# Two attention branches on one core: local projections first, attention blocks spread over two stages, the gate on column tiles, the range test read late

## The chip, the cores and the metric

The kernel runs on one core of a Trainium2 chip. The metric is device time in microseconds (us) of one execution, and fewer is better. Five engines run their own instruction streams: PE (TensorE, matmuls, with its weight loads listed as PEld), DVE (VectorE), ACT (ScalarE), POOL (GpSimd) and SP (SyncE, which here only issues DMAs). PE writes to PSUM, eight banks of 128 x 512 f32 values; ACT and DVE read it out.

## The reference

Two branches read the same x (2048 x 1024) and are mixed by a gate per row. H is 32 heads of 32 columns.

```
g = sigmoid((x * gate_w).sum(-1, keepdims=True))
# A, linear attention:   q, k, v = split(x @ A_wqkv)
phi = lambda t: where(t > 0, t + 1, exp(t)) + 1e-6
kv = phi(k)^T v (32 x 32 per head);   z = sum over rows of phi(k)
a = ((phi(q) @ kv) / (phi(q) @ z + 1e-6)) @ A_wo
# B, local attention:    q, k, v = split(x @ B_wqkv)
each row attends to itself and the 7 rows 2, 4, ... 14 before it, softmax
b = (softmax(q k^T / sqrt(32)) @ v) @ B_wo
out = g * a + (1 - g) * b
```

## The kernel before, in words

Even and odd rows of x are kept apart (the local window steps by two), so that a window is 8 neighbouring rows of one parity. `xT` holds x transposed, 8 slices of 128 features by 2048 rows, in 16 row tiles of 128. Every projection is made of groups: eight matmuls 128x128 by 128x512, one for each feature slice, into one PSUM bank (`group`, L1237). There are 256 groups in all, 2048 such matmuls. `ws` holds four weight slots of 1024 columns (in the profile w_4, w_5, w_6, w_7 for slots 0 to 3), loaded in halves of 512 columns (`load_w`, L1208).

The order of the instructions comes from a planner, `Prog`. Each operation is recorded with its engine, an estimated cost, what it reads and writes, and a priority (by default its place in the program). `schedule` places the operations by these costs, on each engine always the ready one with the lowest priority number, and `emit` writes the five streams in that order with semaphore waits. On the chip each engine then runs its stream strictly in order. PSUM banks are handed out in rotation (`Ring.next`) in program order, before the planner moves anything: a group must wait until the bank it was given has been read out.

The stages of before, in program order:

1. Linear k and v (L1257 to L1291): for each of 16 row tiles four groups. The first also computes the gate's sum with eight extra 128x1 matmuls (L1280). phi on k is three operations (`phi_natural`: ACT Exp L1247, DVE min and add L1248, DVE max and add L1250), v is one ACT copy (L1289). Then 32 small matmuls on column tiles (L1262) add the tile's kv and z into bank 7, which stays open for the whole stage. Six banks rotate.
2. Local v (L1310 to L1324): 32 groups, read out through two `vst` tiles and stored to DRAM, from where the attention blocks load their windows.
3. Fold (L1334 to L1352): the block-diagonal kv is transposed in eight steps and multiplied into A_wo in 16 matmuls, so that later one product with `ws[3]` does both. Three banks rotate.
4. Local k and q (L1418 to L1446): 64 groups, all read out by DVE (L1440, L1442), and 2 x 2 running maxima for the range test (`top`, L1194). From the second quarter on, `slot(0.36)` lets an attention block in about every third group. There are 36 blocks (`fill`). A block is 16 score matmuls on row tiles into banks 4 to 7 (L1380), one Exp on ACT (E, L1385), the mask on DVE (L1388), and two groups later 32 matmuls on column tiles: values into bank 3 and sums into a rotating bank (L1398, L1402); ACT makes Ln and Exp of the sums (L1407, L1408), DVE multiplies (L1409). Only banks 0, 1 and 2 rotate for everything else.
5. Linear q, the numerators (L1455 to L1473): 32 groups with phi and a running maximum; two slots later (`over`) the denominator matmul (L1465), Ln and Exp on ACT (L1467, L1468) and a product on DVE (L1470). Attention blocks go on in between, and three banks still rotate.
6. A's output (L1480 to L1492): 32 groups with the folded weights, read out into the same place, scaled by g (L1489). The last blocks lie in between.
7. The range test (L1496 to L1511): the maxima go through DRAM and back (L1502, L1503) to one partition, and `flag` says whether the fast formulas were safe. Every engine reads it at its very end.
8. B's output (L1515 to L1528): 32 groups, combined on DVE and stored.

Of the kernel before, what the change touches and what calls it, by code (L numbers as in the profile page):

```python
# [24 lines left out]
class Tile:  # L25
# [13 lines left out]
    def all(self):  # L39
        return [(self.space, self.lo, self.lo + self.row * self.size)]  # L40

    def part(self, *idx):
# [12 lines left out]
        return [(self.space, b + lo * self.size, b + hi * self.size) for b in out]  # L55
# [6 lines left out]
class Prog:  # L62
# [14 lines left out]
    def op(self, eng, fn, cost, reads=(), writes=(), prio=None, chan=None, lat=0.0, after=(), name=""):  # L77
# [10 lines left out]
        for sp, lo, hi in rd:  # L88
# [7 lines left out]
        for sp, lo, hi in wr:  # L96
            for rec in self.recs.get(sp, ()):
                if rec[0] < hi and lo < rec[1]:
                    o.deps.add(rec[2])
        o.deps.discard(o)  # L100
        for sp, lo, hi in wr:
            lst = self.recs.setdefault(sp, [])
            lst[:] = [r for r in lst if not (lo <= r[0] and r[1] <= hi)]
            lst.append((lo, hi, o, True))
        for sp, lo, hi in rd:
            self.recs.setdefault(sp, []).append((lo, hi, o, False))
# [59 lines left out]
    def emit(self, block, tail):  # L166
# [8 lines left out]
        for o in order:  # L175
# [891 lines left out]
def build_kernel(nc, A_x, A_wqkv, A_wo, B_x, B_wqkv, B_wo, gate_w, out):  # L1067
# [37 lines left out]
    class Bank:  # L1105
        def __init__(self, i):
            self.i = i
            self.iv = [("P", i, i + 1)]
# [6 lines left out]
    MX = [("M", 0, 1)]  # L1115
    mx_hbm = nc.dram_tensor("mx_hbm", [4, 128], F32)

    def hb(p0, p1):
        return [("H", p0, p1)]
# [13 lines left out]
    gm = SB([128, NT], F32, "gm")  # L1133
    kvbd = SB([128, 8, 128], BF16, "kvbd")
    zbd = SB([128, 8, 128], BF16, "zbd")
    mx = [SB([128, 512 if i == 2 else 1024], BF16, "mx%d" % i) for i in range(3)]
    mx4 = SB([128, 4], F32, "mx4")
    mx1 = SB([1, 4], F32, "mx1")
    flag = SB([1, 1], I32, "flag")
    er = Ring([SB([128, 512], BF16, "e%d" % i) for i in range(3)])  # L1140
    ph = base[0]

    pk = Ring([SB([128, 1024], BF16, "pk%d" % i) for i in range(2)])
    az = Ring([SB([128, H, 33], BF16, "az%d" % i) for i in range(2)])
    vst = Ring([SB([128, 1024], BF16, "vst%d" % i) for i in range(2)])
    top = base[0]

# [4 lines left out]
    base[0] = max(base[0], top)  # L1152
    pr = Ring([SB([128, 512], BF16, "p%d" % i) for i in range(3)])
    kvT = SB([128, 8, 128], BF16, "kvT", at=pr.t[0].lo)
    mxr = SB([1, 4, 128], F32, "mxr", at=pr.t[0].lo)
    RAr = Ring([SB([128, 512], F32, "ra%d" % i) for i in range(2)])
    osb = Ring([SB([128, 1024], BF16, "o%d" % i, at=RAr.t[i].lo) for i in range(2)])
    if base[0] > nc.sbuf_usable_end:
        raise ValueError("SBUF %d over" % (base[0] - nc.sbuf_usable_end))

    mm = lambda n: max(n / 2400.0, 0.0267) + 0.0025
# [25 lines left out]
    for m in mx:  # L1187
        C("dve", lambda e, m=m: e.memset(m[:, :], 0.0), 0.2, [m.all()])

    def top(ms, src, reg, n):  # L1190

        for i, op in zip(ms, (ALU.max, ALU.min)):
            m = mx[i]
            P.op("dve", lambda e, m=m, op=op: e.tensor_tensor(m[:, 0:n], m[:, 0:n], src, op), 0.06 + n / 1920.0, reads=[m.all(), reg], writes=[m.all()])  # L1194
# [7 lines left out]
    def load_x(t, prio):  # L1202
        e_, r = t // 8, t % 8
        return P.op("sp", lambda e: e.dma_start_transpose(xT[:, :, t * 128:(t + 1) * 128], x2[e_, r * 128:(r + 1) * 128, :]),
                    0.3, writes=[xT.part((0, 8), (t * 128, (t + 1) * 128))], prio=prio, chan="x%d" % t, lat=1.3)

    def load_w(slot, half, src, c0, prio, n=512):
        return P.op("sp", lambda e: e.dma_start(ws[slot][:, :, half * 512:half * 512 + n], src[:, :, c0:c0 + n]), 1.4 * n / 512,  # L1208
                    writes=[ws[slot].part((0, 8), (half * 512, half * 512 + n))], prio=prio, chan="w%d_%d" % (slot, half), lat=4.5 * n / 512)
# [6 lines left out]
    load_w(0, 0, Aw, 1024, 1)  # L1216
    P.op("sp", gw_load, 0.6, writes=[gw.all()], prio=1.5, chan="gw", lat=0.5)
    load_w(0, 1, Aw, 1536, 2)
    load_w(1, 0, Aw, 2048, 3)
    load_x(1, 3.5)  # L1220
    load_w(1, 1, Aw, 2560, 4)
    for t in range(2, NT):
        load_x(t, 3 + t)
    load_w(2, 0, Bw, 2048, 20)
    load_w(2, 1, Bw, 2560, 21)
    load_w(3, 0, Ao, 0, 30)
    load_w(3, 1, Ao, 512, 31)
# [357 lines left out]
```

## Time and profile before

| what | value |
|---|---|
| median of 3 runs | 562.78 us (561.68 to 563.06) |
| the profiled execution's own time | 562.65 us |
| its span, first to last instruction | 560.7 us |
| mean granted TensorE clock | 0.98 |
| PE, DVE, ACT busy | 92%, 54%, 36% of the span |

The profile's views give times from the span's start. Busy time of PE is modelled for pipelined matmuls, so two of its figures are of use: start to start of matmuls that follow one another, and stretches where it is not busy at all. A stretch table has, for each engine, its busy time and in brackets its instruction count, then the granted clock, the busy share of the 16 DMA engines and the rate.

### The profile page before, as it was taken

What the parts mean: (1) busy time and instruction counts of PE and PEld (TensorE: products, weight loads), DVE (VectorE), ACT (ScalarE), POOL (GpSimd) and SP (SyncE); (2) the same over time, 40 slices, a digit from 0 to 9 for tenths busy, and PEclk for the clock granted to TensorE, in tenths of its full rate; (3) what the DMA queues carried; (4) which work ended last, traced back from release to release, by engine and by line L of the source; (5) the groups of instructions that cost most, each with busy time, mean ns of one, the idle gap of its engine ahead of it and who ended that gap; (6) DMA issues with size and microseconds to landing.
All of it is one profiled execution on the core that took longest, in us unless ns stands there. A gap on an engine that the chain in (4) does not pass through costs nothing.

```text
span 560.7 us, 10080 instructions
## 1 busy us (share of the span) xinstructions
PE 514.2 (92%) x4472; PEld 230.9 (41%) x4472; DVE 303.4 (54%) x514; ACT 202.5 (36%) x294; POOL 4.7 (1%) x21
## 2 busy tenths in 40 slices
PE   3999999999999789999999998888884999999996
PEld 1444444444444234444444443333331333444443
DVE  1222222224211347788888899888882555634443
ACT  1233232332111210133443469888882355300000
POOL 3000000000000000000000000000000000000000
PEclk9999999999999979999999999999998899999999
DMA  8997000009312600002100030000000011001222
GB/s 242 223 197 240 1 1 2 1 1 305 127 75 76 205 0 1 1 20 95 29 21 20 20 106 11 9 11 20 11 11 10 21 30 29 1 2 68 83 76 78
DMA packets 44948, 34.81 MB, mean 62 GB/s; under 512 B 19809, under 2 KB 40801, under 8 KB 44898
## 3 DMA queue, kind: packets, MB, share of 16 engines
q1 hardware_dynamic: 44898, 34.09, 21.1%
q8 instruction: 37, 0.61, 0.4%
q14 instruction: 13, 0.11, 0.1%
HBM read 21.50 MB, written 8.39 MB: 53 GB/s over the span
## 4 chain that ended last, share of the span: by engine, by line
PE 81%; DVE 8%; ACT 5%; DMA 4%; SPq 1%; issue 1%
PE ps_all L1237 75%; DMA mx_hbm<-mx_22_70 2%; DMA w_5_53<-in_A_wqkv_dram 2%; PE ps_all L1398 2%; PE ps_all L1343 1%; PE ps_all L1380 1%; PE ps_all L1402 1%; PE ps_all L1262 1%; DVE xT_49 L1489 1%; ACT w_7_55 L1349 1%; ACT ra_48_96 L1467 1%; ACT ra_48_96 L1468 1%; DVE xT_49 L1470 1%; DVE p_43_91 L1250 1%; DVE p_44_92 L1250 1%
## 5 line engine op out<-in xcount | busy, mean ns | idle before, releaser
L1237 PE MATMUL ps_all<-w_4_52,xT_49 128*128 128x512 bf16 x256 | 62.5, 383 | 9.7 <-DMA gw_61<-in_gate_w_dram 9.7
L1237 PE MATMUL ps_all<-xT_49,w_6_54 128*128 128x512 bf16 x256 | 60.5, 380 | 9.2 <-ACT ra_48_96 L1467 2.8
L1237 PE MATMUL ps_all<-xT_49,w_4_52 128*128 128x512 bf16 x256 | 59.7, 385 | 0.0
L1237 PE MATMUL ps_all<-w_5_53,xT_49 128*128 128x512 bf16 x256 | 58.0, 380 | 0.8 <-DMA w_5_53<-in_A_wqkv_dram 0.8
L1237 PE MATMUL ps_all<-xT_49,w_5_53 128*128 128x512 bf16 x256 | 58.6, 379 | 0.0
L1237 PE MATMUL ps_all<-w_4_52,qT_50 128*128 128x512 bf16 x256 | 55.9, 379 | 0.4 <-ACT E_36_84 L1385 0.4
L1237 PE MATMUL ps_all<-w_6_54,xT_49 128*128 128x512 bf16 x256 | 55.6, 379 | 0.0
L1237 PE MATMUL ps_all<-w_7_55,xT_49 128*128 128x512 bf16 x192 | 44.4, 380 | 0.4
L1237 PEld LDWEIGHTS ps_all<-w_4_52,xT_49 128*128 128x128 bf16 x256 | 23.9, 98 | 39.1 <-DMA gw_61<-in_gate_w_dram 9.6
L1237 PEld LDWEIGHTS ps_all<-xT_49,w_6_54 128*128 128x128 bf16 x256 | 23.2, 98 | 38.9 <-ACT ra_48_96 L1467 4.5
L1237 PEld LDWEIGHTS ps_all<-w_4_52,qT_50 128*128 128x128 bf16 x256 | 24.8, 98 | 30.6 <-ACT E_36_84 L1385 0.9
L1237 PEld LDWEIGHTS ps_all<-xT_49,w_4_52 128*128 128x128 bf16 x256 | 24.9, 99 | 30.3 <-issue 2.1
L1237 PEld LDWEIGHTS ps_all<-w_6_54,xT_49 128*128 128x128 bf16 x256 | 25.0, 98 | 30.0
L1237 PEld LDWEIGHTS ps_all<-xT_49,w_5_53 128*128 128x128 bf16 x256 | 24.4, 98 | 29.0
L1237 PEld LDWEIGHTS ps_all<-w_5_53,xT_49 128*128 128x128 bf16 x256 | 23.8, 98 | 28.5 <-DMA w_5_53<-in_A_wqkv_dram 1.3
L1385 ACT ACTIVATE E_34_82<-ps_all 128x1824 bf16<-128x1824 f32 x12 | 20.3, 1691 | 33.6 <-PE ps_all L1380 33.6
L1489 DVE TENSOR_SCALAR xT_49<-ps_all,g_63 128x512 bf16<-128x512 f32 x24 | 16.9, 746 | 27.7 <-PE ps_all L1237 27.7
L1407 ACT ACTIVATE L_37_85<-ps_all 128x456 f32<-128x456 f32 (+1 forms) x18 | 9.9, 550 | 54.6 <-PE ps_all L1402 54.6
L1442 DVE CAST kT_51<-ps_all 128x512 bf16<-128x512 f32 x32 | 21.6, 686 | 12.4 <-PE ps_all L1237 12.4
L1248 DVE TENSOR_SCALAR e_25_73<-e_25_73 128x512 bf16<-128x512 bf16 x22 | 6.4, 292 | 39.6 <-ACT e_25_73 L1247 39.6
L1440 DVE TENSOR_SCALAR qT_50<-ps_all 128x512 bf16<-128x512 f32 x32 | 21.6, 685 | 9.8 <-PE ps_all L1237 9.8
L1237 PEld LDWEIGHTS ps_all<-w_7_55,xT_49 128*128 128x128 bf16 x192 | 17.5, 98 | 21.5 <-DVE xT_49 L1489 1.3
(146 smaller groups left out, 608.7 us busy)
## 6 DMA issues: line engine op xcount, KB each, us to landing
w_4_52<-in_A_wqkv_dram SPq DMA_DIRECT2D x2, 1024.0 KB, 8.1
w_5_53<-in_A_wqkv_dram SPq DMA_DIRECT2D x2, 1024.0 KB, 8.3
w_6_54<-in_B_wqkv_dram SPq DMA_DIRECT2D x2, 1024.0 KB, 7.9
w_7_55<-in_A_wo_dram SPq DMA_DIRECT2D x2, 1024.0 KB, 11.7
w_4_52<-in_B_wqkv_dram SPq DMA_DIRECT2D x2, 1024.0 KB, 6.3
w_5_53<-in_B_wqkv_dram SPq DMA_DIRECT2D x2, 1024.0 KB, 8.9
vB_hbm<-vst_32_80 SPq DMA_DIRECT2D x8, 256.0 KB, 2.0
vB_hbm<-vst_33_81 SPq DMA_DIRECT2D x8, 256.0 KB, 2.0
```

The costliest lines, as they stand in the source:

```text
L1237: last = e.matmul(bank.ap(0, n), lhs(dc), rhs(dc), start=(dc == 0), stop=(dc == 7))
L1248: P.op("dve", lambda e: e.tensor_scalar(e_[:, :], e_[:, :], 1.0, 1e-6, op0=ALU.min, op1=ALU.add), 0.25, reads=[e_.all()], writes=[e_.all()])
L1250: P.op("dve", lambda e: e.scalar_tensor_tensor(out=dst, in0=bank.ap(), scalar=0.0, in1=e_[:, :], op0=ALU.max, op1=ALU.add), dps(512), read ...
L1262: last = e.matmul(kvb.ap()[32 * j:32 * j + 32, i * 33:i * 33 + 33], pkt[:, h * 32:(h + 1) * 32], azt[:, h, :], start=False, stop=(t == NT ...
L1343: last = e.matmul(bs[jh].ap(), kvT[:, i, :], ws[3][:, i, jh * 512:(jh + 1) * 512], start=True, stop=True)
L1349: P.op("act", lambda e, dst=dst, b=bs[jh]: e.activation(dst, b.ap(), ACT.Copy), act(512), reads=[bs[jh].iv], writes=[ws[3].part((i, i + 1) ...
L1385: P.op("act", lambda e: e.activation(E[:, :, 0:nq].rearrange("p (j c) q -> p j c q", j=4), ps[:, 4:8, 0:4 * nq].rearrange("p j (c q) -> p ...
L1398: e.matmul(OB.ap(c * nq, (c + 1) * nq)[32 * j:32 * j + 32, :], vt[:, (4 * c + j) * 32:(4 * c + j) * 32 + 32], E[:, 4 * j + c, 0:nq], start ...
L1407: P.op("act", lambda e: e.activation(L[:, 0:4 * nq], db.ap(0, 4 * nq), ACT.Ln), act(4 * nq), reads=[db.iv], writes=[L.all()])
L1440: P.op("dve", lambda e, dst=dst, bank=bank: e.tensor_scalar(dst, bank.ap(), SCALE, None, op0=ALU.mult), dps(512), reads=[bank.iv], writes= ...
L1442: P.op("dve", lambda e, dst=dst, bank=bank: e.tensor_copy(dst, bank.ap()), dps(512), reads=[bank.iv], writes=[reg])
L1489: P.op("dve", lambda e, dst=dst, b=bs[jh], t=t: e.tensor_scalar(dst, b.ap().rearrange("p (i s) -> p i s", s=128), g[:, t:t + 1], None, op0 ...
```

## The change

Nothing is computed differently except where the gate is summed. What moves:

- **Order of the stages.** Local v comes first, then the gate, local k and q, linear k and v, linear q with the fold and A's output woven in, B's output. Linear k/v weights now sit in slots 3 and 0, folded A_wo in slot 1, B_wo in slot 3.
- **The start.** The first weights are cut in pieces (four of 2 feature slices, two of 4) and issued from ACT, while SP issues only x. Nine matmuls on a zeroed tile (`WARM`) run on PE before. Local v uses four `vst` tiles and seven banks. The next weights are issued only after given tiles (`early`).
- **Gate.** `gate_w` is copied into 32 columns per slice, and 32 matmuls of 32 columns by 512 rows on four column tiles (L1313) replace the 128 matmuls 128x1. The sums go through DRAM to change their layout.
- **kv and z.** Each tile's 32 small matmuls go into a rotating bank, and DVE adds that to `kva` in SBUF.
- **Attention blocks.** `slot(FILL)`, 0.34, stands in both the local k/q and the linear k/v loops; all blocks are through before the numerators end. Three banks rotate in both stages. Local k is now read out by ACT.
- **Numerators.** All eight banks rotate. The fold is one transpose batch after the fourth numerator and 2 matmuls after each of the next but two. From the 18th numerator on, each is followed by one group of A's output, whose read-out is shared by DVE and ACT.
- **Range test.** Same chain, with the lowest priority and a longer estimated latency for its DMA.
- **The planner.** Operations on the same engine other than PE now always wait on the semaphore for each other where they depend.

The heart of the diff, in the order of the program (the two `slot(FILL)` are those of local k and q and of linear k and v; the three new rings are those of local v, of both these stages, and of all that follows):

```
-                        slot(0.36)
+                        slot(FILL)
...
+            slot(FILL)
...
-    main = Ring([banks[i] for i in (0, 1, 2, 4, 5, 6)])
-    kvb = banks[7]
+    main = Ring(banks[0:7])
...
+    main = Ring(banks[0:3])
...
+    main = Ring(banks)
...
+    for d in range(0, 8, 2):
+        load_w(0, 0, Bw, 2048, 1, d, d + 2, "act")
+    for d in range(0, 8, 4):
+        load_w(0, 1, Bw, 2560, 2, d, d + 4, "act")
+    for t in range(1, NT):
+        load_x(t, 3 + t)
...
+    for i in range(WARM):
+        P.op("pe", lambda e: e.matmul(banks[7].ap(), warm[:, 0:128], warm[:, :], start=True, stop=True), 0.43, reads=[warm.all()], writes=[banks[7].iv], prio=-1)
...
+                last = e.matmul(gbank.ap()[32 * u:32 * u + 32, :], gwr[:, dc, :], xT[:, dc, u * 512:(u + 1) * 512], start=(dc == 0), stop=(dc == 7),
+                                tile_position=(0, 32 * u), skip_group_check=True)
...
+            P.op("dve", lambda e: e.tensor_tensor(kva[:, :, :], src(), kva[:, :, :], ALU.add), dps(264), reads=[bank.iv, kva.all()], writes=[kva.all()])
...
+    for n, (u, j) in enumerate(nums):
+        numer(u, j)
+        slot(0)
+        if n == 3:
+            turn()
+        if 6 <= n < 14:
+            fold(n - 6, 0)
+            fold(n - 6, 1)
+        if n >= 17:
+            a_out(*outs.pop(0))
+            slot(0)
...
-                    if o.eng == "pe" or (d not in o.raw and o.eng != "pool"):
+                    if o.eng == "pe":
```

Three places show how the instructions stand. The first is PE's stream in the linear k and v stage. Before, k's first half is w_4 and v is w_5; `az`, `pk` are the kv matmuls, `gw` the gate.

```order
L1262 MATMUL ps_all<-az_30_78,pk_28_76 32x33 x32
L1237 MATMUL ps_all<-w_5_53,xT_49 128x512 x16
L1237 MATMUL ps_all<-w_4_52,xT_49 128x512
L1280 MATMUL ps_all<-gw_61,xT_49 128x1
L1237 MATMUL ps_all<-w_4_52,xT_49 128x512
```

Now, with k from w_7 and v from w_4, `qT`, `kT` the scores and `E` the values and sums of attention blocks:

```order
L1354 MATMUL ps_all<-qT_50,kT_51 128x114 x16
L1253 MATMUL ps_all<-w_4_52,xT_49 128x512 x8
L1253 MATMUL ps_all<-w_7_55,xT_49 128x512 x8
L1354 MATMUL ps_all<-qT_50,kT_51 128x112 x16
L1443 MATMUL ps_all<-az_48_96,pk_46_94 32x33 x32
L1372 MATMUL ps_all<-E_35_83,v_38_86 32x114 x16
L1376 MATMUL ps_all<-E_35_83,ones_58 32x114 x16
L1253 MATMUL ps_all<-w_4_52,xT_49 128x512 x8
L1253 MATMUL ps_all<-w_7_55,xT_49 128x512 x8
L1253 MATMUL ps_all<-w_4_52,xT_49 128x512 x8
```

The gate's matmuls are gone from this stage, and blocks stand between its groups: 20 of the 36 scores come after the first linear k group, 16 before it.

The second place is PE's stream among the numerators (xT by w_6). Before, with `zbd` the denominators:

```order
L1237 MATMUL ps_all<-xT_49,w_6_54 128x512 x8
L1398 MATMUL ps_all<-E_35_83,v_39_87 32x114 x16
L1402 MATMUL ps_all<-E_35_83,ones_58 32x114 x16
L1465 MATMUL ps_all<-p_44_92,zbd_66 128x512
L1237 MATMUL ps_all<-xT_49,w_6_54 128x512 x8
L1465 MATMUL ps_all<-p_45_93,zbd_66 128x512
L1237 MATMUL ps_all<-xT_49,w_6_54 128x512 x8
L1380 MATMUL ps_all<-qT_50,kT_51 128x114 x16
```

Now, where A's output (w_5 by pq) has begun:

```order
L1253 MATMUL ps_all<-xT_49,w_6_54 128x512 x24
L1521 MATMUL ps_all<-p_50_98,zbd_67 128x512
L1253 MATMUL ps_all<-w_5_53,pq_8_56 128x512 x8
L1521 MATMUL ps_all<-p_51_99,zbd_67 128x512
L1253 MATMUL ps_all<-xT_49,w_6_54 128x512 x8
L1521 MATMUL ps_all<-p_52_100,zbd_67 128x512
L1253 MATMUL ps_all<-w_5_53,pq_8_56 128x512 x8
```

A numerator and its denominator now stand beside a group of A's output in place of a block.

The third place is DVE's stream around the range test: the last maximum's reduction, the read of the maxima that came back (mxr), and A's output being read out. Before:

```order
L1497 TENSOR_REDUCE mx_22_70<-mx_21_69 128x1
L1470 TENSOR_TENSOR xT_49<-p_43_91,ra_48_96 128x512
L1489 TENSOR_SCALAR pq_8_56<-ps_all,g_63 128x4x128 x2
L1470 TENSOR_TENSOR xT_49<-p_44_92,ra_49_97 128x512
L1505 TENSOR_REDUCE mx_23_71<-mxr_95 1x4
L1489 TENSOR_SCALAR pq_8_56<-ps_all,g_63 128x4x128 x2
```

Now:

```order
L1215 TENSOR_REDUCE mx_21_69<-mx_57_105 128x1
L1547 TENSOR_SCALAR xT_49<-ps_all,g_63 128x4x128
L1525 TENSOR_TENSOR xT_49<-p_52_100,ra_54_102 128x512
L1547 TENSOR_SCALAR xT_49<-ps_all,g_63 128x4x128 x4
L1578 TENSOR_REDUCE mx_22_70<-mxr_91 1x4
L1581 TENSOR_TENSOR mx_22_70<-mx_22_70 1x1 x3
```

Between the reduction and the read that waits for DRAM there were two read-outs, of one row tile; now there are five, each of a row tile of its own (ACT reads the other half).

More of the change, by code (lines that the diff above doesn't have):

```diff
@@ new lines, in build_kernel @@
+    for t in range(NT):
+        pkt, _ = pk.next()
+        azt, _ = az.next()
+        xs, xr = x_tile(t)
+        for r in range(4):
+            bank, _ = main.next()
+            w, wr = w_half((3, 0)[r // 2], r % 2)
+            group(bank, xs, w, [xr, wr])
+            if r < 2:
+                phi(bank, pkt[:, r * 512:(r + 1) * 512], pkt.part((r * 512, (r + 1) * 512)))
+            else:
+                hh = (r - 2) * 16
+                P.op("act", lambda e, bank=bank, azt=azt, hh=hh: e.activation(azt[:, hh:hh + 16, 0:32], bank.ap().rearrange("p (h d) -> p h d", d=32), ACT.Copy),
+                     act(512), reads=[bank.iv], writes=[azt.part((hh, hh + 16), (0, 33))])
+            if r == 3:
+                after(2, lambda t=t, pkt=pkt, azt=azt: state(t, pkt, azt))
+            slot(FILL)
@@ L1493, in build_kernel @@
[L1493 to L1498 removed]
+        bank, _ = main.next()
+        hold[jh] = bank
+        w, wr = w_half(1, jh)
```

402 lines of the change are left out of this document (210 added, 192 removed).

## The prediction

> **What bounds the kernel now.** I read the page's head first, then the stretch table by stage, then the chain of waits, then single operations. In the head, the figure behind x counts instructions.
>
> ```profile
> span 560.7 us, 10080 instructions
> PE 514.2 (92%) x4472; PEld 230.9 (41%) x4472; DVE 303.4 (54%) x514; ACT 202.5 (36%) x294; POOL 4.7 (1%) x21
> ```
>
> PE is the engine that is nearly full. The stretch table says where it is not (columns: stretch, its length, busy time and instructions of PE, PEld, DVE, ACT, POOL, granted clock, DMA share, GB/s).
>
> ```profile
> 0.00:20.00 20.00, 9.50 (x51) 4.09 (x52) 3.21 (x7) 3.50 (x5) 4.71 (x21) 1.00 0.94 252
> 180.00:220.00 40.00, 34.25 (x142) 13.52 (x141) 19.88 (x36) 5.97 (x10) 0.00 (x0) 0.87 0.22 73
> 220.00:320.00 100.00, 100.00 (x1046) 47.15 (x1045) 84.92 (x128) 35.50 (x40) 0.00 (x0) 1.00 0.10 29
> 320.00:420.00 100.00, 87.08 (x861) 37.30 (x858) 87.94 (x165) 82.25 (x126) 0.00 (x0) 1.00 0.08 25
> 420.00:440.00 20.00, 11.18 (x112) 4.68 (x112) 6.27 (x14) 5.87 (x7) 0.00 (x0) 0.74 0.07 15
> 440.00:500.00 60.00, 55.81 (x687) 24.93 (x686) 32.60 (x45) 24.80 (x32) 0.00 (x0) 1.00 0.06 17
> ```
>
> PE is idle 10.5 us at the start, 5.8 in the fold, 12.9 among the numerators, where DVE and ACT are both above 80%, 8.8 while the range test is awaited, and 4.2 in A's output. Local k and q (220 to 320) run at 100% with DVE at 85% and only three banks in rotation. The clock is below 1.00 only where PE has just been idle.
>
> The chain, in order of time, gives the speed of PE when nothing holds it, and the range test's price.
>
> ```profile
> 30.55 0.31 PE ps_all L1262 x32
> 134.27 53.65 PE ps_all L1237 x248
> 235.95 5.29 PE ps_all L1237 x24
> 241.24 0.32 PE ps_all L1398 x15
> 241.56 0.21 PE ps_all L1402 x13
> 241.77 0.31 PE ps_all L1380 x16
> 419.06 10.97 DMA mx_hbm<-mx_22_70
> 430.10 1.99 DMA mxr_95<-mx_hbm
> 556.39 0.75 DVE o_51_99 L1523
> ```
>
> 53.65 / 248 = 0.2163 us for a matmul, so 1.73 for a group of eight. An attention block is 0.53 for values and sums (0.32 + 0.21) and 0.31 for scores; a tile's kv is 0.31. Twenty-four plain matmuls should take 5.19 and took 5.29: going from plain matmuls to small ones costs 0.10, once for each run of small ones.
>
> **The change part by part: PE's work.** I count what PE must do and add what holds it.
> - 2048 plain matmuls x 0.2163 = 443.0.
> - 36 blocks x 0.84 = 30.2, and 16 kv x 0.31 = 5.0. The order has 58 runs of small matmuls now (72 before), x 0.10 = 5.8.
> - 32 denominators and 16 fold products of the same shape, 48 x 0.2163 = 10.4; the eight transposes about 0.6, an estimate from 128 columns in place of 512.
> - The gate: 32 matmuls of 512 columns on four column tiles. Values do 16 of 114 columns on four tiles in 0.21 to 0.32. Scaled by columns that is 0.21 / (16 x 114) x 32 x 512 = 1.9. Were the four tiles to run one after another it would be 32 x 0.2163 = 6.9. I take 2.0, since the values are the same form of matmul.
>
> Together 497.0.
>
> **The start.** These rows are of the timeline (SPq is the time in which SP issues).
>
> ```profile
> 9.65 0.61 PE L1237 MATMUL ps_all<-w_4_52,xT_49 128*128 128x512 bf16 x1 [9.65 <-DMA gw_61<-in_gate_w_dram]
> 13.00 1.89 PE L1237 MATMUL ps_all<-w_4_52,xT_49 128*128 128x512 bf16 x8
> 13.31 23.60 SPq L1204 DMA_TRANSPOSE xT_49<-in_A_x_dram  x14
> 15.74 0.61 PE L1237 MATMUL ps_all<-w_5_53,xT_49 128*128 128x512 bf16 x2 [0.85 <-DMA w_5_53<-in_A_wqkv_dram]
> ```
>
> And two rows of a finer stretch table, columns as above:
>
> ```profile
> 2.00:4.00 2.00, 0.00 (x0) 0.00 (x0) 0.28 (x2) 0.08 (x1) 2.00 (x7) 1.00 0.71 138
> 44.00:48.00 4.00, 4.00 (x50) 1.78 (x49) 1.97 (x4) 1.30 (x3) 0.00 (x0) 1.00 1.10 348
> ```
>
> Before, PE waits for the third half of weights until 15.74, having done two groups: as if it had started at 15.74 - 2 x 1.73 = 12.3 and never stopped. An x tile costs 23.60 / 14 = 1.69; 1 MB of weights at 348 GB/s costs 3.0. Data begins to move at about 2.5 (half of the stretch 2 to 4 at a full rate). Now PE's order is the first weight half with x tiles 0, 1 and 2, then the second half. Both halves and three tiles are 6.0 + 5.1 = 11.1, so the fourth group can start at 13.6 with three done: an effective start of 13.6 - 3 x 1.73 = 8.4. But SP goes on issuing x. With half of the DMA time for each queue, the second MB lands at 2.5 + 2 x 6.0 = 14.5, start 9.3. With three more tiles ahead of it, 13.5. I take 9.5. Before, the first group took 13.00 - 9.65 = 3.35 (with its gate matmuls) where 1.73 is the rule; matmuls on zeros that run ahead can save up to 1.6 of that, and lose it again where PE has to wait. The range holds it. The Trainium skill, page "DMA: Bandwidth & Descriptors", section "Queues, rings and completion order", says that each DMA engine takes turns between the queue rows packet by packet; with equal packets that is the half-and-half case, 9.3, and no run shows two queues yet.
>
> In local v 16 x tiles, four stores and more weights share the DMA. The tile copied fifth waits for the first store, which SP issues after 13 transposes, about 13 x 1.69 + 6.0 + 2.5 = 30 us, when it would be due at 9.5 + 9 x 1.73 = 25. Seven banks let PE run on until its 16th group, at 9.5 + 15 x 1.73 = 35. I take 0; without that cover up to 5.
>
> **What holds PE later.** Durations of single operations (the line that groups them, busy us, then mean ns):
>
> ```profile
> L1385 ACT ACTIVATE E_34_82<-ps_all 128x1824 bf16<-128x1824 f32 x12 | 20.3, 1691 | 33.6 <-PE ps_all L1380 33.6
> L1407 ACT ACTIVATE L_38_86<-ps_all 128x456 f32<-128x456 f32 x16 | 8.8, 552 | 39.4 <-PE ps_all L1402 39.4
> L1408 ACT ACTIVATE L_38_86<-L_38_86 128x456 f32<-128x456 f32 x16 | 9.4, 586 | 0.0
> L1247 ACT ACTIVATE e_25_73<-ps_all 128x512 bf16<-128x512 f32 x22 | 13.2, 601 | 27.3 <-PE ps_all L1237 27.1
> L1467 ACT ACTIVATE ra_48_96<-ps_all,eps_60 128x512 f32<-128x512 f32 x16 | 11.0, 688 | 1.2 <-PE ps_all L1465 1.2
> L1468 ACT ACTIVATE ra_48_96<-ra_48_96 128x512 f32<-128x512 f32 x16 | 10.2, 635 | 0.2
> L1388 DVE TENSOR_TENSOR E_34_82<-E_34_82,msk_59 128x1824 bf16<-128x1824 bf16 x12 | 13.2, 1100 | 1.7 <-ACT E_34_82 L1385 1.7
> L1409 DVE TENSOR_TENSOR qT_50<-ps_all,L_37_85 128x456 bf16<-128x456 f32 x16 | 10.0, 626 | 0.6 <-ACT L_37_85 L1408 0.3
> L1250 DVE SCALAR_TENSOR_TENSOR p_43_91<-ps_all,e_27_75 128x512 bf16<-128x512 f32 x11 | 7.6, 687 | 0.2
> L1248 DVE TENSOR_SCALAR e_25_73<-e_25_73 128x512 bf16<-128x512 bf16 x22 | 6.4, 292 | 39.6 <-ACT e_25_73 L1247 39.6
> L1194 DVE TENSOR_TENSOR mx_21_69<-mx_21_69,p_44_92 128x512 bf16<-128x512 bf16 x11 | 4.6, 421 | 0.2
> L1470 DVE TENSOR_TENSOR xT_49<-p_45_93,ra_49_97 128x512 bf16<-128x512 bf16 x4 | 2.8, 689 | 0.4 <-ACT ra_49_97 L1468 0.4
> ```
>
> And from the timeline two numerators, the first and the fifth of a cycle:
>
> ```profile
> 346.12 1.90 PE L1237 MATMUL ps_all<-xT_49,w_6_54 128*128 128x512 bf16 x8 [0.94 <-DVE p_45_93 L1250]
> 357.01 1.25 PE L1237 MATMUL ps_all<-xT_49,w_6_54 128*128 128x512 bf16 x5 [0.90 <-DVE p_43_91 L1250]
> ```
>
> A block takes 2.83 of ACT and 1.73 of DVE; a numerator with its denominator 1.92 of ACT and 2.09 of DVE against 1.95 of PE. Before, four numerators and a block make one cycle of 357.01 - 346.12 = 10.89: ACT 10.5, DVE 10.1, PE only 8.7. The engines that read PSUM are full there, and PE loses 2.2 a cycle. The change takes the blocks away from the numerators.
> - **Local k and q**, 16 blocks: k's read-out moves to ACT, which was at 35%. Three banks held nobody up with DVE at 85%. I take 1 us lost, between 0 and 4.
> - **Linear k and v**, 20 blocks in 64 groups. Per tile PE needs 6.92 + 0.41 + 1.25 x 0.94 = 8.5; ACT 4 x 0.60 + 1.25 x 2.83 = 5.9 (70%); DVE 2 x 0.98 + 1.25 x 1.73 and the sum into kva, half as wide as L1250's 0.69 and so about 0.5 (an estimate), 4.6 (54%). That lies nearer to the stretch 220 to 320 than to the full cycle, so PE should run; but a phi holds its bank for three operations, and an Exp of 1.69 can stand ahead on ACT. Bounds: 0, and the 2.2 of the full cycle for each of 20 blocks, 44. I take 5.
> - **First 18 numerators**, where the fold's read-outs come too. From the transposes to the first group of A's output PE has 11 groups, 16 products and some 15 denominators, 25.7 with the 0.2163 each; ACT, with its half of the fold's read-outs at 0.60 like L1247, 11 x 0.60 + 15 x 1.32 + 8 x 0.60 = 31. I take 5 lost, between 0 (eight banks carry the arrears into the next stretch) and 8. The new own-engine waits cost DVE a little here and are in that.
> - **Numerators with A's output**: PE 1.95 + 1.73 = 3.68 a pair; a read-out of A's output, about 0.7 like L1250's, falls to each of DVE and ACT every second pair, so DVE 2.4 and ACT 2.3. 1 us, at most 4.
> - **Range test**: reduction 0.7 and two DMAs, 10.97 + 1.99, make 13.7. DVE has five read-outs to do first, one per two groups, 17 us of PE. Cost 0; what it covers before (8.8 idle and a slow clock) goes. The gate's trip through DRAM stands the same way ahead of DVE's read-outs in local k and q; 0, at most 5.
>
> Behind the last matmul before come 560.7 - 556.39 = 4.3; I keep 4.3, though the last store is now half as wide.
>
> **Sum:** 497.0 + 9.5 + 4.3 + 12 (1 + 5 + 5 + 1) = 522.8 of span. The profiled execution took 562.65 for 560.7, so 2.0 lie around the span: 524.8. Its own time is 0.1 below the median, and no correction is due.
>
> **The rivals.**
> - *The banks hold linear k and v up.* Half of the full cycle's loss, 22 in place of 5, gives 541.8. For it: ACT's 1.69 ahead of a phi. Against: 100% of PE with three banks at 220 to 320. Chance 0.13.
> - *The start or local v is bound by DMA*: start 13.5, 5 for stores and 5 for the gate, 524.8 + 14 = 538.8. For it: the rate of 1.69 per x tile. Against: seven banks and a store every 3.5 us. Chance 0.08.
> - *Slower: the clock falls in linear k and v.* If the small waits there idle PE enough for the clock to drop to the 0.74 of 420 to 440, the stage's 16 x 8.5 = 136 us become 184, 48 more: 572.6. It decides from 0.78 on (37.9 more is the time before). Against: at 320 to 420 PE was idle for 13% in small waits with the clock at 1.00. Chance 0.04. The Trainium skill, page "TensorE: Matmul & The Clock Gate", section "A second HAM failure mode: psum-queue depth-cycling", describes such a loss from short idles between groups that cycle through PSUM banks. By that rule it would happen; the trace speaks against it, and the 0.74 came after one wait of several us.
> - *The range test still stops DVE*: its read is in the middle of A's output, and if the trip took 22 us instead of 13.7, A's read-outs would stand for 5: 529.8, inside the range, and part of the first case's chance.
>
> **The numbers.** My forecast, 525, has 0.75, with its own range 513 to 535 (start 8 to 12, losses 2 to 20). The first two rivals have 0.21, reaching 541.8. The range 513 to 541 leaves out less than 2 in 10. Differences under 0.3% are about what a measurement of this kernel can tell from none. Slower has 0.04 from the clock, plus 0.01 for the rivals together; the same 0.01; faster 0.94.
>
> **What would show it.** In the profile after: first plain matmul near 7 us and no wait over 3 us afterwards in local v; stretches of PE at 100% through local k and q; in linear k and v a period of 8.5 to 8.9 per tile at clock 1.00 (10 or more would be the bank rival, a clock under 0.9 the slower one); ACT over 90% in the 25 us before A's output; the read of mxr with no idle DVE time that PE then waits for. A PE idle total above 50 us, or a clock below 0.95 outside the start, would make the forecast wrong.

## The result: 520.0 us, and the profile after

Over four runs each, the changed kernel takes 520.01 us (519.46 to 520.46) and the kernel before 562.23 us (560.69 to 563.06). The ratio is 0.925, with an interval of 0.923 to 0.928. The prediction was 525, with 513 to 541 as its range. The profiled execution took 520.42 us for a span of 518.7. Two of the four runs, this one among them, had a mean granted clock of 0.99 and took 520.4 and 520.5 us; the other two had 1.00 and took 519.5 and 519.6.

The page's head, with the figure behind x for counts. PE is idle for 14.3 us now (518.7 - 504.4), where it was idle for 46.5. So 32.2 of the 42.0 us by which the span fell are idle time of PE, and 9.8 are busy time (514.2 - 504.4), which was not taken apart further.

```profile
span 518.7 us, 9927 instructions
PE 504.4 (97%) x4385; PEld 229.8 (44%) x4385; DVE 276.3 (53%) x477; ACT 232.0 (45%) x342; POOL 4.7 (1%) x21
```

The stretch table by stage: the start, the rest of local v, local k and q (two rows), linear k and v, the numerators with the fold, those with A's output, and the rest of A's with B's output.

```profile
0.00:20.00 20.00, 14.83 (x48) 5.24 (x49) 1.93 (x4) 3.07 (x4) 4.68 (x21) 0.83 1.01 210
20.00:67.00 47.00, 47.00 (x219) 21.11 (x216) 9.98 (x15) 7.16 (x12) 0.00 (x0) 1.00 0.92 246
69.00:100.00 31.00, 31.00 (x145) 14.02 (x144) 16.04 (x27) 6.35 (x11) 0.00 (x0) 1.00 0.34 106
100.00:195.00 95.00, 95.00 (x1107) 44.20 (x1106) 68.02 (x100) 53.95 (x68) 0.00 (x0) 1.00 0.17 54
195.00:335.00 140.00, 137.64 (x1980) 65.17 (x1982) 73.68 (x127) 88.69 (x125) 0.00 (x0) 1.00 0.11 32
346.00:371.00 25.00, 22.61 (x107) 9.41 (x105) 24.70 (x55) 22.67 (x42) 0.00 (x0) 1.00 0.00 1
383.00:431.40 48.40, 48.40 (x226) 21.93 (x225) 31.76 (x62) 28.16 (x47) 0.00 (x0) 1.00 0.00 1
431.40:514.40 83.00, 82.90 (x385) 37.32 (x382) 32.08 (x49) 7.23 (x11) 0.00 (x0) 1.00 0.13 49
```

Two stretches are left in which PE is not full behind the start: linear k and v, and the 25 us before A's output, where DVE is busy for 24.70 of 25.00. The list of PE's waits says the same with names (us in total, times, the longest; two rows of the start are left out):

```profile
PE ps_all L1253 <- DMA w_4_52<-in_B_wqkv_dram: 3.0, 2, 2.1
PE ps_all L1253 <- ACT ra_54_102 L1523: 1.8, 3, 1.1
PE ps_all L1253 <- DVE pk_46_94 L1262: 0.7, 1, 0.7
PE ps_all L1253 <- DVE pk_47_95 L1262: 0.7, 1, 0.7
PE ps_all L1521 <- DVE p_51_99 L1262: 0.5, 1, 0.5
PE ps_all L1253 <- ACT L_37_85 L1381: 0.3, 1, 0.3
PE ps_all L1253 <- DVE kva_68 L1451: 0.2, 1, 0.2
```

The `pk`, `L` and `kva` rows are those of linear k and v, 1.9 in all; the `ra` and `p` rows are those of the first numerators, 2.3. Before, one wait for DVE in A's output alone was 7.7. The chain gives the ends of the stages:

```profile
10.87 56.21 PE ps_all L1253 x250
67.08 1.84 PE ps_all L1313 x32
431.42 82.89 PE ps_all L1253 x384
514.34 0.75 DVE o_56_104 L1597
```

The last 384 matmuls run at 0.2159 us each without a stop. The 250 of local v took 0.2248 each: something slowed them, and the start's own part below shows what.

For the range test, SP's issues and DVE's rows around its read, from the timeline:

```profile
430.91 0.37 SPq L1575 DMA_DIRECT2D mx_hbm<-mx_21_69  x1
439.19 0.27 SPq L1577 DMA_DIRECT2D mxr_91<-mx_hbm  x1
445.27 0.75 DVE L1547 TENSOR_SCALAR xT_49<-ps_all,g_63 128x512 bf16<-128x512 f32 x1 [2.70 <-PE ps_all L1253]
445.94 0.66 DVE L1578 TENSOR_REDUCE mx_22_70<-mxr_91 1x4 f32<-1x512 f32 x1
```

The read (L1578) follows a read-out of A's output with no idle time ahead of it. The trip itself was still 8 us for the first DMA alone.

### The profile page after: what moved, and what is told of

Its sections match the earlier page's. It is cut to its first block, busy times and chain, and to the rows that moved or that the text cites. A ratio compares the mean times of both kernels' runs of the same rounds, so it can differ in the third digit from the quotient of the medians.

```text
span 518.7 us, 9927 instructions
## 1 busy us (share of the span) xinstructions
PE 504.4 (97%) x4385; PEld 229.8 (44%) x4385; DVE 276.3 (53%) x477; ACT 232.0 (45%) x342; POOL 4.7 (1%) x21
## 4 chain that ended last, share of the span: by engine, by line
PE 92%; DVE 5%; DMA 2%; ACT 1%; ACTq 0%; issue 0%
PE ps_all L1253 84%; PE ps_all L1354 2%; PE ps_all L1372 2%; DMA w_4_52<-in_B_wqkv_dram 2%; PE ps_all L1376 1%; PE ps_all L1443 1%; PE ps_all L1521 1%; DVE mx_57_105 L1211 1%; DVE w_5_53 L1281 1%; DVE pq_8_56 L1525 1%; DVE pq_8_56 L1262 1%; PE ps_all L1313 0%; ACT e_27_75 L1259 0%; DVE xT_49 L1525 0%; DVE kva_68 L1451 0%; DVE e_27_75 L1260 0%
## 5 line engine op out<-in xcount | busy, mean ns | idle before, releaser
L1253 PE MATMUL ps_all<-w_7_55,qT_50 128*128 128x512 bf16 x256 | 55.4, 379 | 0.0
L1279 ACT ACTIVATE kT_51<-ps_all 128x512 bf16<-128x512 f32 x32 | 19.1, 597 | 60.5 <-PE ps_all L1253 60.5
L1359 ACT ACTIVATE E_33_81<-ps_all 128x1824 bf16<-128x1824 f32 x12 | 20.2, 1687 | 4.7 <-PE ps_all L1354 4.6
L1211 DVE TENSOR_TENSOR mx_44_92<-mx_44_92,kT_51 128x1024 bf16<-128x1024 bf16 x16 | 11.0, 690 | 21.1 <-ACT kT_51 L1279 21.1
L1359 ACT ACTIVATE E_34_82<-ps_all 128x1824 bf16<-128x1824 f32 x12 | 20.2, 1686 | 2.1 <-PE ps_all L1354 2.1
L1359 ACT ACTIVATE E_35_83<-ps_all 128x1824 bf16<-128x1824 f32 (+1 forms) x12 | 20.1, 1677 | 2.1 <-PE ps_all L1354 2.1
L1259 ACT ACTIVATE e_25_73<-ps_all 128x512 bf16<-128x512 f32 x22 | 13.1, 596 | 17.4 <-PE ps_all L1253 17.4
L1451 DVE TENSOR_TENSOR kva_68<-ps_all,kva_68 128x264 f32<-128x264 f32 x15 | 6.5, 433 | 26.3 <-PE ps_all L1443 26.3
L1362 DVE TENSOR_TENSOR E_35_83<-E_35_83,msk_59 128x1824 bf16<-128x1824 bf16 (+1 forms) x12 | 13.2, 1100 | 12.4 <-ACT E_35_83 L1359 12.4
L1259 ACT ACTIVATE e_26_74<-ps_all 128x512 bf16<-128x512 f32 x21 | 12.5, 597 | 15.9 <-PE ps_all L1253 15.9
## 6 DMA issues: line engine op xcount, KB each, us to landing
w_4_52<-in_A_wqkv_dram SPq DMA_DIRECT2D x2, 1024.0 KB, 10.1
```

The source lines that it names most:

```text
L1253: last = e.matmul(bank.ap(), lhs(dc), rhs(dc), start=(dc == 0), stop=(dc == 7))
L1259: P.op("act", lambda e: e.activation(e_[:, :], bank.ap(), ACT.Exp), act(512), reads=[bank.iv], writes=[e_.all()])
L1279: P.op("act", lambda e: e.activation(dst, bank.ap(), ACT.Copy), act(512), reads=[bank.iv], writes=[reg])
L1359: P.op("act", lambda e: e.activation(E[:, :, 0:nq].rearrange("p (j c) q -> p j c q", j=4), ps[:, 4:8, 0:4 * nq].rearrange("p j (c q) -> p ...
L1362: P.op("dve", lambda e: e.tensor_tensor(E[:, :, 0:nq], E[:, :, 0:nq], msk[:, mi:mi + 1, 0:nq].to_broadcast([128, 16, nq]), ALU.mult), 0.15 ...
L1451: P.op("dve", lambda e: e.tensor_tensor(kva[:, :, :], src(), kva[:, :, :], ALU.add), dps(264), reads=[bank.iv, kva.all()], writes=[kva.all()])
```

## Experiments

Each kernel is the changed one with one edit or two, timed beside the kernel before. The changed kernel itself, run once more beside the last group, is the yardstick:

> The changed kernel once more, beside these runs on the same chip: 519.3 to 520.5 us by every theory.

It took 520.22 us (519.01 to 521.02), ratio 0.923 (0.921 to 0.925). Differences of a microsecond from that are not told apart here.

### The range test read early, with eight banks and with three

```diff
-    P.op("sp", mx_out, ..., chan="mxo", lat=8.0, prio=1e5)
+    P.op("sp", mx_out, ..., chan="mxo", lat=0.5)
```

(and so for the other operations of the test). The second kernel has this line as well, ahead of the groups of A's output that follow the numerators:

```diff
+    main = Ring([b for b in banks if b is not hold[0]][0:3])
```

> The changed kernel with the range test put back where its order had it: default priority and a short estimated latency, so that DVE's read of the returned maxima stands behind two read-outs of A's output after the reduction, in place of five. Theory (eight rotating banks cover the trip, whatever stands ahead of the read): DVE is kept from about 435.7 to 441.5, one read-out comes 3 to 4 us late, PE has eight banks of 1.73 each to go on with, so 520 to 521 us. Rival (the late read is what removed the 8.8 us of idle PE of before): the idle comes back, with the slow clock behind it, 526 to 535 us.

> The early range test as in the run beside it, and only three banks in rotation for the groups of A's output that follow the numerators. Theory (the banks are the cover): a read-out that is 4 us late lets PE go on for two groups of 1.73 and then stops it for 1 to 3 us, 521 to 523 us, and PE shows a wait for DVE's read-out there that the run with eight banks does not show. Rival (the order of DVE alone decides): the same time as with eight banks, within 1 us.

With eight banks 519.30 us (518.68 to 521.37): no cost. With three banks 526.82 us (526.32 to 527.16), ratio 0.936 (0.933 to 0.938) against 0.922 (0.919 to 0.924), so 7.5 us. From the timelines, DVE's read in the first, and in the second DVE's read and then PE's rows:

```profile
443.88 0.67 DVE L1578 TENSOR_REDUCE mx<-mxr 1x4 f32<-1x512 f32 x1 [7.46 <-DMA mxr<-mx_hbm]
```

```profile
442.20 0.68 DVE L1580 TENSOR_REDUCE mx<-mxr 1x4 f32<-1x512 f32 x1 [7.39 <-DMA mxr<-mx_hbm]
```

```profile
430.41 8.80 PE L1253 MATMUL ps_all<-w,xT 128*128 128x512 bf16 x40
443.78 1.03 PE L1253 MATMUL ps_all<-w,xT 128*128 128x512 bf16 x2 [4.57 <-DVE mx L1583]
```

DVE waits just as long in both, 7.4 us. With eight banks PE never waits for it; with three PE stops 4.4 us after DVE does (at 430.41 + 8.80 = 439.21, against 442.20 - 7.39 = 434.81), for 4.57. The two profiled executions differ by 4.95 (521.37 and 526.32), and this wait is nearly all of that; what makes the medians differ by more was not found. So the banks are a cover of their own, and the late read is not what the gain needs. The Trainium skill, page "Perfetto Trace Analysis", section "Matmul Optimizations", advises to make use of all eight banks; here the trace agrees, with 4.57 us of idle PE for three and none for eight.

### Few banks among the numerators

```diff
-    main = Ring(banks)
+    main = Ring(banks[0:3])
...
+        if n == 17:
+            main = Ring(banks[3:7])
```

> The changed kernel with three banks in rotation for the first 17 numerators and the fold, and four for the numerators that A's output is paired with, in place of eight; no blocks are among them. Theory of the prediction (what held the numerators before was ACT and DVE being full with the blocks, and the banks only carry arrears): 2 to 6 us more, 522 to 526 us. Rival (three banks were what held the numerators before): before lost 2.2 us for each four numerators, so 17.6 us for 32, 536 to 540 us.

526.01 us (525.44 to 526.32), 5.8 more than the control. The stretch from 346 to 395 of this kernel and of the changed one:

```profile
346.00:395.00 49.00, 41.99 (x179) 17.01 (x182) 39.63 (x78) 36.09 (x63) 0.00 (x0) 1.00 0.00 1
```

```profile
346.00:395.00 49.00, 46.61 (x218) 20.24 (x216) 43.97 (x95) 40.48 (x72) 0.00 (x0) 1.00 0.00 1
```

With few banks PE is idle for 7.0 in place of 2.4, while DVE and ACT are *less* busy in the same time. So the loss is time in which groups wait for a bank, and no added work of the engines that read it. The 5.8 lies at the upper end of what the theory gave and far from the rival's 17.6.

### Where the later blocks stand

In the first kernel the 20 blocks leave linear k and v and go among the numerators; in the second the Exp of each denominator is left out as well, so that its output is no longer the function asked for. In both, A's output comes wholly behind the numerators, and three banks rotate until the last block is through.

```diff
-            slot(FILL)
-    while todo or later:
-        slot(1.0)
+            slot(0)
+    while later:
+        slot(0)
...
         numer(u, j)
-        slot(0)
+        slot(0.45)
```

```diff
-            P.op("act", lambda e: e.activation(R[:, :], R[:, :], ACT.Exp, scale=-1.0), ...)
```

> The changed kernel with the 20 later blocks taken out of linear k and v and put among the numerators and A's output (0.45 of a block for each group), where three banks rotate until the last block is through. Theory (ACT and DVE are full there with blocks): 20 blocks bring 56.6 us of ACT to a stage in which ACT then has 122 us of work by the mean durations and PE 115; with the 2.2 us that each four numerators lost before, 8 x 2.2 = 17.6, so 530 to 542 us, and linear k and v without any wait. Rival (where the blocks stand does not matter, since PE has the same work): 518 to 521 us.

> The run with the 20 later blocks among the numerators (543.3 us), with the Exp on ACT of each denominator left out: the product takes the logarithm itself. ACT has 32 x 0.63 = 20 us less to do, DVE and PE as much as before, and no bank is held less long by itself, since Ln has read it. Theory (ACT's queue, 86% busy there, is what holds PE): 525 to 533 us. Rival (the three banks and the way of a block through them hold it): 538 to 543 us.

543.31 us (541.64 to 544.55) and 535.26 us (534.29 to 536.68), so 23.1 and 15.0 more than the control. The stretch with the numerators, in the one and in the other:

```profile
330.00:415.00 85.00, 65.63 (x603) 28.11 (x600) 67.47 (x126) 70.89 (x115) 0.00 (x0) 0.96 0.05 13
```

```profile
328.00:410.00 82.00, 65.97 (x676) 29.21 (x686) 70.54 (x135) 60.21 (x92) 0.00 (x0) 1.00 0.05 16
```

Taking 20 us of work from ACT gave back 8 of the 23. ACT was busy for 83% of the stretch and is busy for 73%, DVE for 79% and 86%, PE for 77% and 80%. The run lies between the two expectations (525 to 533, 538 to 543), so each holds in part: ACT's queue is one share of what blocks cost among the numerators, and the rest was not taken apart. No single engine is full there. Two things are mixed in: three banks without any blocks cost 5.8 above, so the 23.1 are not the blocks' alone; and the granted clock is 0.96 in the first stretch and 1.00 in the second, so some of the 8 may be clock.

### How densely the blocks stand in linear k and v

First a block after every group in place of every third; then the same with one wait more on ACT.

```diff
-            slot(FILL)
+            slot(1.0)
```

```diff
-             reads=[s.iv for s in SO], writes=[E.all()])
+             reads=[s.iv for s in SO], writes=[E.all()], after=last_exp[-1:])
```

> The changed kernel with the 20 blocks of linear k and v let in after every group in place of every third, so that they are over after five row tiles. Theory (ACT bounds a tile with four blocks): such a tile has ACT 2.4 + 4 x 2.83 = 13.7 us, DVE about 9.4 and PE 11.1 by the mean durations, so 2.6 us a tile, 8 to 13 us in all, 528 to 533 us. Rival (PE has the same work, and nothing but PE bounds the stage): 519 to 521 us. If mean durations overstate ACT, since one operation begins before the one ahead has ended, the loss is smaller: with 0.1 us less for each of 16 operations 1.0 us a tile, 5 us in all, 525 us.

> The run with a block after every group of linear k and v (550.7 us), with one wait added on ACT: the long Exp of a block's scores stands behind Ln and Exp of the sums of the block two before it, in place of between them. Theory (a block's way is bound by a chain: values into the one value bank, Ln, the next block's long Exp of 1.69, Exp of the sums, product on DVE, and only then the next values; 4.5 to 5.1 us a block in that run's trace against 2.9 of PE, so 1.6 x 20 = 32 us lost): with the 1.69 out of the chain ACT's own 3.3 us a block bounds it, 0.4 to 0.9 us x 20, so 528 to 538 us. Rival (ACT or DVE is simply full): 547 to 552 us, since their work is the same.

550.67 us (550.03 to 550.77): 30.5 more than the control, where 5 to 13 had been expected from ACT's work. That theory fell, and the trace says how. The stretch 215 to 300, and then, from the timeline, the way of one block and the values of the next two (rows of other work left out):

```profile
215.00:300.00 85.00, 62.52 (x1141) 29.57 (x1140) 36.63 (x56) 53.17 (x71) 0.00 (x0) 0.94 0.08 23
```

```profile
219.72 0.39 PE L1372 MATMUL ps_all<-E,v 128*32 128x114 bf16 x16 [1.30 <-DVE qT L1383]
220.37 0.55 ACT L1381 ACTIVATE L<-ps_all 128x456 f32<-128x456 f32 x1 [1.92 <-PE ps_all L1376]
220.82 1.69 ACT L1359 ACTIVATE E<-ps_all 128x1824 bf16<-128x1824 f32 x1
220.98 3.59 PE L1253 MATMUL ps_all<-w,xT 128*128 128x512 bf16 x8 [0.66 <-ACT L L1381]
222.39 0.58 ACT L1382 ACTIVATE L<-L 128x456 f32<-128x456 f32 x1
222.54 1.11 DVE L1362 TENSOR_TENSOR E<-E,msk 128x1824 bf16<-128x1824 bf16 x1 [2.87 <-ACT E L1359]
223.56 0.63 DVE L1383 TENSOR_TENSOR qT<-ps_all,L 128x456 bf16<-128x456 f32 x1
224.81 0.39 PE L1372 MATMUL ps_all<-E,v 128*32 128x114 bf16 x16
229.33 0.39 PE L1372 MATMUL ps_all<-E,v 128*32 128x114 bf16 x16 [1.05 <-DVE qT L1383]
```

And the longest of the same kernel's waits of PE (us in total, times, the longest):

```profile
PE ps_all L1372 <- DVE qT L1383: 12.6, 11, 1.3
```

Nobody is full: PE 74%, ACT 63%, DVE 43%. But the values of a block go into one bank, and the next block's values must wait until the product (L1383) has read it. That product waits for two things: the Exp of the sums (L1382), which stands behind the next block's long Exp (L1359) on ACT, and the mask of that same next block (L1362), which the long Exp releases and which stands ahead of the product on DVE. The mask ends last, at about 223.6, and the product begins. From values to values it is 4.64 us on the mean of five. The pair at 219.72 and 224.81 is the longest, 5.09: the group between them ran at half speed and kept PE to 224.57, so the second values did not wait for the product; the next ones, at 229.33, did. With the wait that puts the long Exp behind both short operations the kernel takes 529.85 us (528.75 to 531.35), 20.8 less, with the same work and inside what the theory gave. Values then follow each other in 3.1 to 3.2 in these rows:

```profile
214.49 0.39 PE L1373 MATMUL ps_all<-E,v 128*32 128x114 bf16 x16
217.68 0.39 PE L1373 MATMUL ps_all<-E,v 128*32 128x114 bf16 x16
220.80 0.39 PE L1373 MATMUL ps_all<-E,v 128*32 128x114 bf16 x16
```

and a stretch of the same kernel reads

```profile
205.00:245.00 40.00, 30.96 (x724) 16.47 (x727) 25.85 (x38) 37.22 (x48) 0.00 (x0) 1.00 0.14 42
```

ACT is at 93% now, and only now is it nearly full. So it was a chain that cost the 20.8, not a full engine. Some of it came by way of the clock, which is 0.94 in the first stretch and 1.00 in this one; 0.06 of 85 us is 5, an estimate of the most that this can be there.

### The pairs of numerator and A's output

```diff
-        if n >= 17:
-            a_out(*outs.pop(0))
-            slot(0)
```

> The changed kernel with A's output wholly behind the numerators, not woven in from the 18th on. Theory (by the mean durations a numerator needs DVE 2.09 and PE 1.95): DVE bounds the last 15 numerators, 0.14 us each, 2 us and some arrears of the fold, 521 to 525 us. Rival 1 (operations overlap on DVE, start to start a numerator needs 1.73 there): PE bounds them, 520 to 521 us. Rival 2 (the pairing is what took the numerators' loss of before away, 0.55 us each): 528 us.

519.30 us (519.05 to 522.24): no difference. Without blocks, and with the fold's arrears over, a numerator by itself keeps PE full (24.00 of 24.00 us from 371 to 395 in this kernel, with DVE at 23.52); the first rival was right.

### The start

Without the matmuls on zeros; with more of them, between the pieces of weights; and with a wait as well that was meant to hold back x tiles 3 and on.

```diff
-    WARM = 9
+    WARM = 0
```

```diff
+                    for i in range({4: 4, 6: 8}[d]):
+                        o = P.op("pe", lambda e: e.matmul(banks[7].ap(), warm[:, 0:128], warm[:, :], ...), ..., after=[o])
```

```diff
-        load_x(t, 3 + t)
+        load_x(t, 3 + t, [w0] if t == 3 else [])
```

> The changed kernel without the nine matmuls on zeros at the start. Theory (the clock has fallen again by the time that PE works without a stop, since PE waits three times, 3.9 us in all, between 5 and 11 us): the matmuls on zeros gain little, 0 to 1 us more, 520 to 521 us, and the granted clock is 0.5 to 0.6 from 10 to about 15 us as it is with them. Rival (they bring the clock up for the first groups): 1.6 us or more is lost as in the first group of before, 521.6 to 524 us.

> The changed kernel with more matmuls on zeros: 11 ahead, 4 between the second and the third piece of weights and 8 between the third and the fourth, where PE waits for DMA. Theory (at the start 1.3 to 2.1 us go to a clock of 0.5 to 0.7 from 8 to 16 us, after the waits): the clock stays at 1.00 and the first stage ends at about 65 us in place of 67.1, 518 to 519.5 us. Rival (the slow clock has another cause, or the added matmuls delay the groups as much as they save): 520 us or more, with the clock below 0.8 between 8 and 14 us.

> The run with more matmuls on zeros, and x tiles 3 to 15 issued only when the first half of the second 1 MB of weights has landed. Theory (at the start the first weights share the DMA with x tiles that are not needed yet; the runs so far have an effective start of 10.7 to 11.3): both halves of weights and three x tiles need 11.1 us from 2.5 on, the first stage ends 1 to 2 us earlier, at 64 to 65 us, and the time is 518 to 519 us. Rival (the gap in x after the wait costs as much as was saved): 520 to 522 us, with PE waiting for x between 14 and 20 us.

519.38 us (519.28 to 520.13), 519.99 us (519.44 to 520.67) and 519.57 us (519.36 to 519.93): none differs from the control by what these runs can tell. The last edit does not do what its expectation says. Only the fourth x tile gets the wait, and the planner then puts seven tiles that have none ahead of it, so SP issues x without a pause:

```profile
0.80 24.68 SPq L1225 DMA_TRANSPOSE xT<-in_A_x_dram  x13
```

PE's first rows in the changed kernel and the stretch behind them, then PE's rows in the kernel without matmuls on zeros, and one in the last kernel:

```profile
1.26 3.89 PE L1284 MATMUL ps_all<-warm_72 128*128 128x512 bf16 x9 [1.26 <-DVE warm_72 L1203]
6.02 1.04 PE L1253 MATMUL ps_all<-w_4_52,xT_49 128*128 128x512 bf16 x4 [0.88 <-DMA xT_49<-in_A_x_dram]
7.99 0.78 PE L1253 MATMUL ps_all<-w_4_52,xT_49 128*128 128x512 bf16 x2 [0.93 <-DMA w_4_52<-in_B_wqkv_dram]
10.87 13.48 PE L1253 MATMUL ps_all<-w_4_52,xT_49 128*128 128x512 bf16 x52 [2.10 <-DMA w_4_52<-in_B_wqkv_dram]
```

```profile
8.00:16.00 8.00, 5.90 (x17) 1.91 (x18) 0.00 (x0) 1.19 (x2) 0.00 (x0) 0.57 1.19 263
```

```profile
5.92 2.72 PE L1253 MATMUL ps_all<-w,xT 128*128 128x512 bf16 x6 [5.92 <-DMA xT<-in_A_x_dram]
10.37 2.33 PE L1253 MATMUL ps_all<-w,xT 128*128 128x512 bf16 x10 [1.73 <-DMA w<-in_B_wqkv_dram]
14.25 15.93 PE L1253 MATMUL ps_all<-w,xT 128*128 128x512 bf16 x73 [1.55 <-DMA xT<-in_A_x_dram]
```

```profile
13.97 26.29 PE L1254 MATMUL ps_all<-w,xT 128*128 128x512 bf16 x118 [1.35 <-DMA xT<-in_A_x_dram]
```

The changed kernel's profiled execution had six matmuls done when it went on at 10.87, an effective start of 10.87 - 6 x 0.2163 = 9.6. It waits for no x tile after that, but it lost 2.1 to a clock of 0.57. Without the matmuls on zeros the first six took 0.45 each, those from 10.37 on ran at their usual speed, and PE waits for an x tile until 14.25 with 16 done, an effective start of 10.8. In the last kernel the wait for that tile, the third, ends at 13.97. So at a full clock the third x tile holds the start up, and where the clock is slow, the slow matmuls fill most of the time of that wait: local v ends between 65.9 and 67.1 us in the profiles of this section. Whether the x tiles behind it and the weights delay that tile on the DMA stays open, since no run held them back.

The slow clock is no fixed part of this start. Ten of the kernels here share the changed kernel's start, with nine matmuls on zeros. From 8 to 16 us the granted clock reads 0.57 to 0.92 in eight of their profiles and 1.00 in two (the early read with eight banks, and the long Exp behind both short operations). It reads 1.00 in the three with another start.

What the own-engine waits cost was not tried.

## Why the prediction was right, step by step

The terms of the sum, and what the profile gives for each (us of span):

| term | predicted | measured |
|---|---|---|
| effective start | 9.5 | 11.7 (67.08 - 256 x 0.2163) |
| local v, 256 matmuls | 55.4 | 55.4 (256 x 0.2163, taken as given) |
| gate | 2.0 | 1.84 |
| PE's other work | 439.6 | 441.2 (514.34 - 68.92 - 4.2) |
| lost to waits | 12 | 4.2 |
| behind the last matmul | 4.3 | 4.36 |
| span | 522.8 | 518.7 |

The span was forecast 4.1 too high: the waits 7.8 too high, the start 2.2 and PE's other work 1.6 too low. So part of the nearness is errors that cancel.

- **PE's work** is right to 0.4%. The gate ran on four column tiles side by side as the values do; that choice, 2.0 out of 1.9 to 6.9, held.
- **The start** is the term that was too low, by 2.2. The step took the second MB of weights as the last thing that PE waits for, with three groups done by then. In the kernel without matmuls on zeros what comes last is the third x tile, at 14.25, with two groups done. In the profiled execution of the changed kernel a clock of 0.57 from 8 to 16 stands in its place. The saving allowed for matmuls on zeros (up to 1.6, "and lose it again where PE has to wait") is lost again: without them the time is the same.
- **Local v and the gate's trip** cost 0, as taken.
- **Local k and q** lost 0 (1 was taken): 95.00 of 95.00 busy with k on ACT.
- **Linear k and v** lost 1.9, where 5 was taken between 0 and 44. A tile takes 8.81 us there (the mean of ten, from the kv matmuls at 222.76 to those at 310.84), inside the 8.5 to 8.9 that was named. The size was fair; the reason given was too weak. The prediction argued from the busy share of ACT and DVE (70% and 54%). The dense run has ACT at 63% and DVE at 43% and loses 30 us. What the two dense runs point to is the distance of one block from the next, by count three groups with the block's own 0.84 and kv's share, about 6.3 us (3 x 1.73 + 0.84 + 0.31), against 4.6 us of the chain through the one value bank. In the changed kernel's timeline the values follow each other after 4.5 to 11.4 us in this stage, 6.8 on the mean, and never wait for the product; a group apart they do. No spacing between these two was tried. The rival "the banks hold linear k and v up", with 22 us, was one of spacing: it is one number in the planner's pace away.
- **First 18 numerators** lost 2.3 (5 was taken, between 0 and 8). ACT was over 90% as foreseen, with 22.67 of 25.00, but DVE, whose work the prediction did not add up there, was fuller still with 24.70. With few banks the kernel loses 5.8 more, so that "eight banks carry the arrears" is shown.
- **Numerators with A's output** lost 0. The pairing has no part in the gain, as the run without it shows.
- **Range test**: cost 0, as taken, and the read came with no wait of DVE. The reason given (five read-outs ahead of it) is enough but not needed: an early read costs nothing with eight banks and 7.5 us with three.
- **"The engines that read PSUM are full there"**, said of numerators with blocks, is half shown. It rested on sums of mean durations, 10.5 and 10.1 of 10.89, while the prediction's own stretch 320 to 420 has DVE busy for 87.94 and ACT for 82.25 of 100. Putting the blocks back, with three banks, costs 23 us, and three banks alone cost 5.8, so taking the blocks away is still the largest part of the gain that was tried. But PE's idle time came with ACT at 83% and DVE at 79%, and 20 us less of ACT's work returned 8.
- **The slower rival**, a clock that falls in linear k and v, did not come: 1.00 in that stage. In the dense run the granted clock was 0.94 from 215 to 300, and the group at 220.98 took 3.59 for eight matmuls, twice the usual. The Trainium skill, page "TensorE: Matmul & The Clock Gate", section "A second HAM failure mode: psum-queue depth-cycling", describes a clock that swings when PE is idle for short times between groups that cycle through PSUM banks. The dense run agrees in that the clock fell in a stage with PE idle for 26%, though the slow group came behind waits of 2.24 and 1.30 us. With the long Exp behind both short operations PE was idle for 23% (30.96 of 40.00 busy) in waits of up to 1.1 us, and the clock stayed at 1.00; in the changed kernel, with PE at 98%, it did too.

The parts do not add up to the 42 us by single undoings: 23 for the blocks with three banks, 6 for the banks alone, 7.5 for early read and few banks together, nothing for the pairing, the matmuls on zeros and the late read by themselves. The order of the stages, the gate on column tiles, kv's sum on DVE and local k's read-out on ACT were not undone, so what each is worth stays open. No version tried beats the changed kernel by more than these runs can tell.

## What to carry to other kernels

In this kernel the blocks, which feed the side engines, lost 1.9 us where PE had three groups to do between two of them, and 23 to 30 where they were crowded or stood among other work for the same engines. So ask how long one piece's own chain of bank, short operations and queues is, and set the distance to more than that. A busy share of 63% says nothing against such a chain. Eight rotating banks hid a stall of 7.4 us on one reading engine, and three did not, so count the banks before reordering reads.

## What the runs showed of the hardware that was not expected

- Where a short ACT operation on the way to freeing a bank stands behind a 1.69 us one in ACT's queue, and the product on DVE behind a mask of 1.11 us that waits for the same long one, 20 blocks took 20.8 us more; an added wait, which only orders ACT's queue, took that away.
- Nine matmuls on zeros ran at 0.43 us each (3.89 for nine), half of the later speed, and after waits of 0.88, 0.93 and 2.10 us the granted clock was 0.57 from 8 to 16. Without them, six matmuls took 2.72 and, after waits of 1.73 and 1.55 us, the rest ran at full speed. With the same nine the clock of that stretch was 1.00 in two of ten profiles, so the matmuls on zeros do not settle it; what does stays open.
